# Output products, x and sums on halves of the array's columns between the transposes of batch 1's pairs

## Chip, cores, metric

One core of one Trainium2 chip. The metric is the device time of one execution in microseconds (us). All runs named here were with a granted clock (the share of TensorE's full clock) of 0.998 to 1.0. Engines: PE is TensorE, PEld its weight loads, ACT ScalarE, DVE VectorE, POOL GpSimd. A product has weights (lhsT, loaded by an instruction of its own) and a moving operand (rhs; in the trace of before, a whole-array product with 512 columns of it takes 0.216 us to the next one, with 288 columns 0.1225). P is the PSUM, in banks, where the products' results are written.

## The reference, cut to what matters

```python
# q, k, v: [8 batches, 8 heads, 576 tokens, 64]
kv = np.einsum('bhsd,bhse->bhde', k, v)
out = np.einsum('bhsd,bhde->bhse', q, kv)
rms = np.sqrt(np.mean(out * out, axis=-1, keepdims=True) + 1e-06)
x = out / rms * g_norm                  # then as [4608 tokens, 512]
y = ((x @ w_a) * (x @ w_b)) @ w_out     # w_a, w_b: 512 x 1536, w_out: 1536 x 512
```

## The kernel before

The heads go in pairs (64 + 64 rows). The tokens of the second stage go in strips of 512. While the output product of strip 0 runs (groups g = 0 to 3 of 128 tokens, 12 products of 512 columns each), the kernel prepares batch 1 in between: a piece of six products, then a step of each of the pairs that are under way. In the names, kv and qtr make the kv product and the transposes of q of a pair, x the product of q with it (`out` in the reference), psq its squares, pss the sums of these, and pst the normalized result. A product on a half uses 64 of the array's 128 columns (128\*64 in the profile's lines, where a whole one has 128\*128) and writes 64 output rows.

```python
def kv(self, p, o):                      # on halves: output rows 0-63 or 64-127
    for c, n in enumerate(rows):         # 6 for batch 1
        for j in range(2):
            nc.tensor.matmul(o[j * D : (j + 1) * D, :],
                lhsT=kk[0:n, 2 * p + j, c, :], rhs=vv[0:n, 2 * p + j, c, :], ...)

def qtr(self, p, i):                     # transposes, on halves too
    for c in range(EC):                  # 6
        for j in range(2):
            nc.tensor.transpose(t[j * D : (j + 1) * D, c, :],
                qt[self.b][:, 2 * p + j, c, :], ident[0:EP, 0:EP])
# ...
O, X, SS = 3, (4, 0), 6                  # PSUM banks; transposes and kv use bank 2
h1, h2 = range(0, FC // 2), range(FC // 2, FC)
ffn_o(0, 0, X[0])
pieces = [(1, h1), (1, h2), (2, h1), (2, h2), (3, h1), (3, h2)]
for n, (g, fcs) in enumerate(pieces):
    o_mm(0, g, O, fcs)                   # 6 products, full array
    if fcs is h2:
        o_out(0, g, O)                   # ACT or DVE copies bank O out
    if 0 <= n - 2 < NP:                  # NP = 4 pairs
        A.pss(n - 2, SS)                 # sums: 2 products, full array; then rs on ACT
        A.pst(n - 2, X[n % 2])           # DVE
    if 0 <= n - 1 < NP:
        A.x(n - 1, X[(n - 1) % 2])       # 2 products, full array
        A.psq(n - 1, X[(n - 1) % 2])     # square, ACT
    if n < NP:
        A.qtr(n, 2)
        A.kv1(n, 2)
        A.kv_out(n, P[:, 2, STRIP - D :])   # ACT
        A.qtr_out(n, 2)                     # DVE
```

## Time and profile before

| | kernel before |
|---|---|
| time | 315.76 us, median of 3 (315.75 to 315.96) |
| PE busy | 98% of the span |
| from the first transposes of batch 1 to the first product of strip 1 | 39.39 to 50.41 us: 11.02 us |

The last row is the stretch that the change touches, called "the stretch" from here on. It is read off the timeline, as the start of the first group of transposes and the start of the first group of products with wa_t after it.

### The profile page before, as it was taken

The numbers are of one execution on the slowest core, as the hardware profiler recorded it, in microseconds if no ns is written. First come the engines' busy times: TensorE is split into PE (matmuls) and PEld (weight loads), VectorE is DVE, ScalarE is ACT, GpSimd is POOL, SyncE is SP. The second block draws the span as 40 slices with busy tenths as digits, with TensorE's granted clock in tenths as the row PEclk, the third lists the DMA queues.
The fourth block names the chain that finished last, engine by engine and source line by source line (L and its number), as shares of the span: only waits on it lengthen the run. The fifth ranks groups of instructions, "written<-read, shape, count | busy, mean of one in ns | idle before, by whom it ended". The sixth has DMA issues, their size and how long they took to land.

```text
span 313.9 us, 4977 instructions
## 1 busy us (share of the span) xinstructions
PE 308.9 (98%) x1907; PEld 147.9 (47%) x1907; DVE 141.6 (45%) x235; ACT 115.9 (37%) x225; POOL 101.2 (32%) x123
## 2 busy tenths in 40 slices
PE   8999999999999999999999999999999999999995
PEld 3544454444445444544454445544544444444443
DVE  4544335456337703583377123761683134214321
ACT  3643255453246313451364024622651233123310
POOL 8954990282453730148138200320230000000000
PEclk9999999999999999999999999999999999999999
DMA  8999999999899999059999980073022200030002
GB/s 181 196 196 199 201 186 166 230 136 152 165 162 184 103 199 151 2 58 162 212 120 130 158 186 2 19 159 109 3 50 60 102 0 0 33 102 1 0 34 101
DMA packets 94253, 36.19 MB, mean 115 GB/s; under 512 B 64918, under 2 KB 89750, under 8 KB 94230
## 3 DMA queue, kind: packets, MB, share of 16 engines
q0 software_dynamic: 59120, 18.44, 54.3%
q1 hardware_dynamic: 34642, 16.87, 24.7%
q10 hardware_dynamic: 468, 0.57, 0.6%
q8 instruction: 15, 0.25, 0.3%
q14 instruction: 8, 0.07, 0.1%
HBM read 37.78 MB, written 12.98 MB: 162 GB/s over the span
## 4 chain that ended last, share of the span: by engine, by line
PE 98%; ACT 1%; issue 0%; DVE 0%
PE P L315 60%; PE P L372 30%; PE P L265 2%; PE P L400 2%; PE P L168 2%; PE P L192 1%; PE P L219 1%; PE P L206 0%; ACT sq L215 0%; PE P L245 0%; PE P L458 0%; ACT o_end L610 0%; PE P L462 0%; PE P L474 0%; DVE zeros L411 0%
## 5 line engine op out<-in xcount | busy, mean ns | idle before, releaser
L333 DVE TENSOR_TENSOR ab<-P,asb 128x512 bf16<-128x512 f32 x108 | 74.5, 691 | 103.6 <-PE P L315 86.0
L315 PE MATMUL P<-xt,wa_t 128*128 128x512 bf16 x432 | 111.9, 380 | 0.0
L315 PE MATMUL P<-xt,wb_t 128*128 128x512 bf16 x432 | 111.7, 379 | 0.0
L329 ACT CAST asb<-P 128x512 bf16<-128x512 f32 x108 | 63.0, 585 | 92.7 <-PE P L315 92.7
L372 PE MATMUL P<-wo_t,ab 128*128 128x512 bf16 (+1 forms) x444 | 95.8, 374 | 0.0
L372 PEld LDWEIGHTS <-ab 128*128 128x128 bf16 x444 | 43.0, 98 | 48.6
L315 PEld LDWEIGHTS <-wa_t 128*128 128x128 bf16 x432 | 41.4, 98 | 47.4 <-issue 0.2
L315 PEld LDWEIGHTS <-wb_t 128*128 128x128 bf16 x432 | 41.5, 98 | 46.9
L288 POOL TENSOR_TENSOR sqt<-rst,g_all 128x512 f32<-128x512 f32 (+1 forms) x24 | 25.0, 1043 | 96.2 <-ACT rst L281 96.2
L385 ACT COPY osb<-P 128x512 f32<-128x512 f32 x17 | 9.9, 585 | 67.3 <-PE P L372 57.5
L387 DVE COPY osb<-P 128x512 f32<-128x512 f32 x18 | 12.4, 691 | 44.1 <-PE P L372 39.5
L139 POOL DMA_DIRECT2D qs<-in_q_dram x12 | 19.8, 1653 | 0.7 <-issue 0.3
L276 DVE TENSOR_REDUCE sst<-sqt 128x8 f32<-128x512 f32 (+1 forms) x24 | 16.3, 680 | 1.8 <-ACT sqt L272 1.1
L297 DVE TENSOR_TENSOR qv<-P,sqt 128x512 bf16<-128x512 f32 (+1 forms) x24 | 16.4, 685 | 0.3
L272 ACT ACTIVATE sqt<-P 128x512 f32<-128x512 f32 (+1 forms) x24 | 14.4, 599 | 4.2 <-PE P L265 4.1
L265 PEld LDWEIGHTS <-qT 128*128 128x128 bf16 x120 | 9.2, 98 | 7.1
L265 PE MATMUL P<-kvb,qT 128*128 128x128 bf16 x120 | 11.6, 219 | 0.0
L281 ACT ACTIVATE rst<-sst,eps_t 128x8 f32<-128x8 f32 (+1 forms) x30 | 9.0, 300 | 4.6 <-DVE sst L276 4.3
L233 DVE SCALAR_TENSOR_TENSOR xt<-P,g_col,rs 128x288 bf16<-128x288 f32 x16 | 7.5, 512 | 5.2 <-ACT rs L223 5.2
L288 POOL TENSOR_TENSOR k_x<-rst,g_all 128x512 f32<-128x512 f32 x6 | 6.3, 1042 | 8.8 <-ACT rst L281 8.8
L131 POOL DMA_DIRECT2D wo_t<-in_moe_w_out_dram x12 | 6.4, 530 | 6.7 <-DMA wb_t<-in_moe_w_b_dram 3.2
L400 PE MATMUL P<-zeros 128*128 128x512 bf16 x17 | 7.2, 568 | 1.2 <-DVE eps_t L417 1.2
(67 smaller groups left out, 119.4 us busy)
## 6 DMA issues: line engine op xcount, KB each, us to landing
out_dram<-osb SPq DMA_DIRECT2D x23, 256.0 KB, 2.1
qs<-in_q_dram POOLq DMA_DIRECT2D x12, 288.0 KB, 7.0
ktl<-in_k_dram POOLq DMA_DIRECT2D x6, 512.0 KB, 9.2
vtl<-in_v_dram POOLq DMA_DIRECT2D x6, 512.0 KB, 11.9
out_dram<-osb SPq DMA_DIRECT2D x13, 128.0 KB, 2.4
wo_t<-in_moe_w_out_dram POOLq DMA_DIRECT2D x12, 128.0 KB, 6.0
wa_t<-in_moe_w_a_dram POOLq DMA_DIRECT2D x5, 256.0 KB, 9.0
wb_t<-in_moe_w_b_dram POOLq DMA_DIRECT2D x5, 256.0 KB, 9.6
```

Source lines behind the costliest of these rows:

```text
L139: nc.gpsimd.dma_start(out=d[:, hs, :], in_=q[b, hs].rearrange("h t d -> t h d"))
L265: nc.tensor.matmul(P[:, i, p * 128 : (p + 1) * 128], lhsT=self.qT[:, p, t0 : t0 + 128], rhs=kvb[self.b % 2][:, p, :], start=True, stop=True,)
L272: nc.scalar.activation(sqt[c % 3][r], self.by_head(i)[r], AF.Square)
L276: nc.vector.reduce_sum(sst[c % 3][r], sqt[c % 3][r], axis=mybir.AxisListType.X)
L288: nc.gpsimd.tensor_mul(sqt[c % 3][r], rst[c % 3][r].unsqueeze(2).to_broadcast([n, H, D]), g_all[r].unsqueeze(1).to_broadcast([n, H, D]),)
L297: nc.vector.tensor_mul(t[r], self.by_head(i)[r], sqt[c % 3][r])
L315: nc.tensor.matmul(self.a if w is wa_t else self.b, lhsT=w[:, kc, self.fc * 128 : (self.fc + 1) * 128], rhs=xt[:, kc, t0 : t0 + STRIP], st ...
L329: nc.scalar.copy(self.t, self.a)
L333: nc.vector.tensor_mul(abt[self.s % 2][self.fc], self.b, self.t)
L372: nc.tensor.matmul(P[:, i, e0:e1], lhsT=abt[s % 2][fc][:, g * 128 : (g + 1) * 128], rhs=wo_t[:, fc, e0:e1], start=(fc == 0), stop=(fc == F ...
L387: nc.vector.tensor_copy(t, P[:, i, :])
L400: nc.tensor.matmul(P[:, i, 0:cols], lhsT=zeros[:, 0:128], rhs=zeros[:, 0:cols], start=True, stop=True)
```

## The change

The intent: TensorE pays something each time it changes between the whole array and halves of its columns (0.09 us or a little more each way in this trace, as the prediction works out). The transposes and the kv products run on halves (their outputs are 64 rows). If the products between them run as two on halves as well, TensorE stays in halves from the first transposes to the last kv products.

```diff
+    def product(o, lhsT, rhs, halves=False, **kw):
+        for r in (slice(0, D), slice(D, 2 * D)) if halves else (slice(0, 2 * D),):
+            nc.tensor.matmul(o[r], lhsT=lhsT[:, r], rhs=rhs, **kw)
... (pss, x and o_mm call product and take halves)
     for n, (g, fcs) in enumerate(pieces):
-        o_mm(0, g, O, fcs)
+
+        halves = 0 < n < NP
+        o_mm(0, g, O, fcs, halves=halves)
...
-            A.pss(n - 2, SS)
+            A.pss(n - 2, SS, halves=halves)
...
-            A.x(n - 1, X[(n - 1) % 2])
+            A.x(n - 1, X[(n - 1) % 2], halves)
```

More of the change, by code (lines that the diff above doesn't have):

```diff
@@ L215, in psq, with pss @@
             nc.scalar.activation(sq[p % 3], P[:, i0 : i0 + 2, 0:HF], AF.Square)
-        def pss(self, p, i0, hs=(0, 1)):
+        def pss(self, p, i0, hs=(0, 1), halves=False):
             for h in hs:
-                nc.tensor.matmul(
-                    P[:, i0 + h, 0:HF], lhsT=ones, rhs=sq[p % 3][:, h, :], start=True, stop=True
+                product(
+                    P[:, i0 + h, 0:HF], ones, sq[p % 3][:, h, :], halves, start=True, stop=True
                 )
@@ L240, in pst, with x @@
                 )
-        def x(self, p, i0):
+        def x(self, p, i0, halves=False):
             for h in range(2):
-                nc.tensor.matmul(
+                product(
                     P[:, i0 + h, 0:HF],
-                    lhsT=kvb[self.b % 2][:, p, :],
-                    rhs=self.qT[:, p, h * HF : (h + 1) * HF],
+                    kvb[self.b % 2][:, p, :],
+                    self.qT[:, p, h * HF : (h + 1) * HF],
+                    halves,
                     start=True,
@@ L368, with o_mm @@
     n_o = [0]
-    def o_mm(s, g, i, fcs, e0=0, e1=d_model):
+    def o_mm(s, g, i, fcs, e0=0, e1=d_model, halves=False):
         for fc in fcs:
-            nc.tensor.matmul(
+            product(
                 P[:, i, e0:e1],
-                lhsT=abt[s % 2][fc][:, g * 128 : (g + 1) * 128],
-                rhs=wo_t[:, fc, e0:e1],
+                abt[s % 2][fc][:, g * 128 : (g + 1) * 128],
+                wo_t[:, fc, e0:e1],
+                halves,
                 start=(fc == 0),
```

## The prediction

> **What bounds the kernel now.** I read the page first: the busy shares and the chain that ended last. Both say that TensorE is the bound.
>
> ```profile
> PE 308.9 (98%) x1907; PEld 147.9 (47%) x1907; DVE 141.6 (45%) x235; ACT 115.9 (37%) x225; POOL 101.2 (32%) x123
> ...
> PE 98%; ACT 1%; issue 0%; DVE 0%
> ```
>
> The reader is to see that a TensorE stretch saved anywhere is saved at the end, unless another engine then makes TensorE wait. The list of waits bears this out: it shows no long TensorE wait after the first 16 us. So I went to the timeline of the stretch that the diff touches, about 39 to 51 us, where pieces of the output product (six 512-column products each) alternate with the preparation of batch 1's four pairs. The first column is the start of a group of products.
>
> ```profile
> 41.26 0.41 PE L245 MATMUL P<-qT,kvb 128*128 128x288 bf16 x2
> 41.60 0.45 PE L192 MATMUL P<-ident,qt 96*64 96x96 bf16 x12
> 41.88 0.35 PE L168 MATMUL P<-vt,kt 96*64 96x64 bf16 x12
> 42.16 1.47 PE L372 MATMUL P<-wo_t,ab 128*128 128x512 bf16 x6
> 43.47 0.41 PE L219 MATMUL P<-sq,ones 128*128 128x288 bf16 x2
> 43.72 0.41 PE L245 MATMUL P<-qT,kvb 128*128 128x288 bf16 x2
> 44.05 0.45 PE L192 MATMUL P<-ident,qt 96*64 96x96 bf16 x12
> 44.33 0.35 PE L168 MATMUL P<-vt,kt 96*64 96x64 bf16 x12
> 44.62 1.47 PE L372 MATMUL P<-wo_t,ab 128*128 128x512 bf16 x6
> 45.93 0.41 PE L219 MATMUL P<-sq,ones 128*128 128x288 bf16 x2
> 46.17 0.41 PE L245 MATMUL P<-qT,kvb 128*128 128x288 bf16 x2
> ...
> 60.86 0.82 PE L168 MATMUL P<-vtl,ktl 128*64 128x64 bf16 x40
> 61.62 0.61 PE L315 MATMUL P<-xt,wa_t 128*128 128x512 bf16 x2
> ```
>
> Two things are to be read from the starts. First, the switch. Two 288-column products take 0.245 us when another full-array product follows (43.47 to 43.72), but 0.33 to 0.34 when the half-array transposes follow (43.72 to 44.05, 41.26 to 41.60): 0.09 for going into halves. For coming out, take the half-array products of L168: 40 of them last 0.76 us to the next group, 12 of them 0.29 (44.33 to 44.62). The 28 more cost 0.47, which is 0.034 per pair, so 12 alone should take 0.20 and 0.09 is left for going back. In the single records of the trace the first group after each switch is also late by a little, 24 ns going in and 10 ns coming out, as its next weight load was not ahead. With those I count 0.117 in and 0.113 out, 0.23 for a round trip. Check: six at 0.216, 0.245 twice, 12 transposes at 0.255 and 12 products at 0.18 sum to 2.22, and the period from 42.16 to 44.62 is 2.46, so 0.24 is over.
>
> Second, halves run side by side. Twelve transposes of 96 columns take 0.28 us (41.60 to 41.88), that is 0.043 per pair after the first, while 96 columns alone need about 0.043 by the rate of the full products (512 in 0.216, 288 in 0.1225). In the single records the partner starts 3 ns later and the next pair 40 ns after that. The moving operand of both partners is the same identity, so reading one operand twice costs nothing there.
>
> [...] The trace has 110 ns for a 64-column load against 98 for a 128-column one. Under a product of 216 or 122 ns it stays hidden; even pairs of 64-column products follow each other every 32 ns.
>
> **The change part by part.** The order of TensorE's instructions was compared as built: 56 rows more, which is 28 weight loads and 28 products. They are 18 of the output product (three pieces of six, n = 1 to 3), 4 of the sums (n = 2, 3) and 6 of x (n = 1 to 3). ACT and DVE have as many instructions as before.
>
> What is removed: before, TensorE goes into halves and out again at each of n = 0 to 3, eight switches. After, it goes in before the transposes of pair 0 and out after the products of pair 3, two switches. Three round trips of 0.23 fall away: 0.69 us.
>
> What is added: 28 partners at about 3 ns, at most 0.08 us, and much less if the pairs overlap across their edges as the transposes do. I take 0.02.
>
> What comes back as waits: the period shrinks from 2.46 to 2.24, and ACT and DVE work between TensorE's steps has a fixed length. I followed it by record.
>
> ```profile
> 41.46 0.58 ACT L385 COPY osb<-P 128x512 f32<-128x512 f32 x1 [0.97 <-PE P L372]
> ...
> 43.92 0.74 ACT L223 ACTIVATE rs<-P,eps_t 128x576 f32<-128x576 f32 x1 [1.01 <-PE P L219]
> 44.55 0.64 ACT L215 ACTIVATE sq<-P 128x576 bf16<-128x576 f32 x1
> 45.09 0.41 ACT L179 CAST kvb<-P 64x64 bf16<-64x64 f32 x2
> ```
>
> ```profile
> 45.55 0.45 DVE L199 COPY qT<-P 128x576 bf16<-128x576 bf16 x1
> ```
>
> (a) The bank of the output product. At n = 1 a group ends and ACT copies it out; the next group (n = 2) writes the same bank and waits for ACT. The last product of the group starts at 41.26 - 0.216 = 41.045, the copy ends at 41.46 + 0.585 = 42.045, and a TensorE product waiting for ACT started 52 ns after ACT's end where I found one (9.465 to 9.517). So the next group can't start before 1.05 us after the last product of the group before. Now it comes at 42.165, 1.12 later, and just misses the wait. After the change TensorE gets there in 0.216 + 0.245 + 0.255 + 0.185 = 0.90. A wait of 0.15 us.
>
> (b) x(2) at n = 3. The sums of pair 0 start at 43.47; behind them ACT does rs, the square of pair 1 and the cast of kvb, then DVE copies qT, done at 46.00; with 52 ns that is 2.58 after the sums' start. TensorE takes 0.245 + 0.245 + 0.255 + 0.185 + 1.295 + 0.245 = 2.47 between the two after the change (2.70 before). A wait of 0.11 us.
>
> The other meetings keep room by the same reckoning: x(1) about 0.2 us (helped by wait (a)), x(3) about 0.1 us as the last switch out lies before it, the bank at n = 4 about 0.1. They are close, so a few hundredths may be wrong.
>
> Sum: 0.69 - 0.02 - 0.15 - 0.11 = 0.41 us gained on TensorE. Nothing behind the stretch seems able to take it back, since TensorE stays busy to the end and transfers wait for it rather than it for them. 315.76 - 0.41 = 315.35 us.
>
> **The rivals.** *Halves of long products run one after the other.* Then 18 x 0.216 + 10 x 0.1225 = 5.1 us come on top and the time is about 320.2, 1.4% slower. For it: no pair in this trace streams 512 columns, and both partners read the same 128 rows. Against it: the transposes share their moving operand too, and pairs of 288 columns on quarters (L206) start 3 ns apart. I give it 4%.
>
> *No wait takes anything back*, because ACT and DVE start earlier than I reckon: 0.67 gained, 315.1. For it: ACT's records overlap by about 0.1 us, so its sums are rough. Against it: each of the two waits hangs on one chain of operations without idle time between them.
>
> *The waits take all of it*, and TensorE is paced by ACT with a period of about 2.4: nothing gained, 315.7. For it: ACT does 0.74 + 0.64 + 0.42 and DVE 0.94 + 0.45 in a row in each period, and DVE's qT copy waits for ACT's cast. Against it: the longest loop is the 2.58 of (b), and it is set against a TensorE path of 2.47, not of 2.24.
>
> *Weight loads show*[...]: a few ns on each of 28 pairs, 0.1 to 0.2 us, so 315.5. Against it are the pairs of 64 columns every 32 ns.
>
> **Range and chances.** The repeated times lie within 0.2 us. The rivals that leave halves side by side span 315.1 to 315.7; with that noise I take 315.0 to 315.8. Two per cent would be 6.3 us, more than eight times all switches that go away, and more than halves one after the other would cost. So within 2% has 0.975, slower 0.015 (halves in sequence, with loads exposed as well), faster 0.01.
>
> **What would show each step right or wrong.** In the timeline after: groups of 12 products for the output at n = 1 to 3 that still take 1.3 us from their start to the next group (2.6 would be the first rival); no 0.09 between x and the transposes at n = 1, 2, 3, and none between the products of L168 and the output group at n = 0, 1, 2; one switch in and one out left. At n = 2 a gap of about 0.15 ahead of the output group, and at n = 3 about 0.1 ahead of x, both laid to ACT or DVE. The stretch from the first transposes to the first product of strip 1 (39.39 to 50.41, 11.02 us) should be about 10.6. The prediction is wrong if that stretch shrinks and the span doesn't, or if the long pairs have another pace than the short ones.

## More of the kernel before

As TensorE is busy to the end, what the stretch loses the span loses too, if nothing else steps in. Its ends, and the first kv products in it:

```profile
39.39 0.45 PE L192 MATMUL P<-ident,qt 96*64 96x96 bf16 x12
39.67 0.35 PE L168 MATMUL P<-vt,kt 96*64 96x64 bf16 x12
...
50.41 0.81 PE L315 MATMUL P<-xt,wa_t 128*128 128x512 bf16 x3
```

More lines of it are in the prediction.

## The result, and the profile after

| | median us | runs | mean us |
|---|---|---|---|
| before | 315.75 (315.67 to 316.1) | 6 | 315.83 |
| after | 315.57 (315.2 to 315.64) | 6 | 315.51 |

The ratio is 0.999, 95% interval 0.9977 to 1.0003. A ratio is the mean time of one kernel's runs over that of the other's of the same rounds, so it is not quite the ratio of the medians. The means differ by 0.32 us, less than the 0.41 forecast, and by the interval not clear of zero.

The chain that ended last was almost all TensorE before (98%). After, the profile's page shows another part in it (the second trace of the same kernel, after_again, has PE 94%, DMA 2%):

```profile
PE 86%; DMA 7%; POOL 4%; issue 1%; ACT 0%; POOLq 0%
```

The timeline of TensorE in the stretch, after. (All products made by the new helper are at L156. The transposes are L197 and the kv products L173.)

```profile
39.23 0.45 PE L197 MATMUL P<-ident,qt 96*64 96x96 bf16 x12
39.79 0.38 PE L173 MATMUL P<-vt,kt 96*64 96x64 bf16 x12
39.97 1.49 PE L156 MATMUL P<-wo_t,ab 128*64 128x512 bf16 x12
41.27 0.44 PE L156 MATMUL P<-qT,kvb 128*64 128x288 bf16 x4
41.52 0.45 PE L197 MATMUL P<-ident,qt 96*64 96x96 bf16 x12
42.01 0.38 PE L173 MATMUL P<-vt,kt 96*64 96x64 bf16 x12
42.19 1.49 PE L156 MATMUL P<-wo_t,ab 128*64 128x512 bf16 x12
...
43.98 0.45 PE L197 MATMUL P<-ident,qt 96*64 96x96 bf16 x12
44.24 0.38 PE L173 MATMUL P<-vt,kt 96*64 96x64 bf16 x12
44.43 1.49 PE L156 MATMUL P<-wo_t,ab 128*64 128x512 bf16 x12
45.73 0.44 PE L156 MATMUL P<-sq,ones 128*64 128x288 bf16 x4
46.10 0.44 PE L156 MATMUL P<-qT,kvb 128*64 128x288 bf16 x4
...
50.25 0.81 PE L321 MATMUL P<-xt,wa_t 128*128 128x512 bf16 x3
```

What is to be seen: twelve half products of 512 columns take 1.30 us to the next group, as six whole ones did. The switches are gone: x to transposes is 0.25 (41.27 to 41.52) where it was 0.34, and kv to the output group is 0.18 (42.01 to 42.19) where it was 0.28 or 0.29. But the transposes of pair 0 now last 0.56 to the kv products (39.23 to 39.79) and those of pair 1 last 0.49, where both took 0.28. That wait is not in the prediction. The chain of waits, cut to the same stretch in order of time, names it:

```profile
34.41 5.33 DMA vt<-in_v_dram
39.74 0.04 issue
39.79 0.38 PE P L173 x12
...
41.96 0.04 issue
42.01 0.38 PE P L173 x12
```

The kv products wait for the v rows of their pair: 34.41 + 5.33 = 39.74, and they start 0.04 later. The same landings, read from the records of the transfers, against the start of the kv products (us):

| kernel | pair 0: landed, started | pair 1 | pair 2 | pair 3 |
|---|---|---|---|---|
| before | 39.51, 39.67 | 41.73, 41.88 | 43.98, 44.33 | 46.17, 46.79 |
| after | 39.74, 39.79 | 41.96, 42.01 | 44.20, 44.24 | 46.40, 46.60 |

Before, the v rows had come 0.15 us ahead of their use for pairs 0 and 1, which leaves 0.11 to spare with the 0.04 from a landing to the start. The stretch after is 39.23 to 50.25, again 11.02 us in this trace. Its waits are 0.28 (v, pair 0), 0.24 (v, pair 1) and 0.12 (x at 46.10, predicted as 0.11), 0.64 in sum, about what the switches gave (0.69).

By the order of the program, the wait at pair 0 is not the change's doing: the first product that the change touches comes after the kv products of pair 0. Of the kernels below that alter nothing up to there either, halves_o waits there (39.33 to 39.76) and switch_more does not (39.47 to 39.75); of the kernel before there is one trace, without the wait. So the stretch mixes the change with a wait that comes and goes from trace to trace. From the first kv products to the first product of strip 1 the traces agree: before 10.74 (39.67 to 50.41; early_before too, 39.27 to 50.01), after 10.46 (39.79 to 50.25; after_again 39.75 to 50.21 and second_bank 39.64 to 50.10 too). That is 0.28 us gained. From there to the end of the span all ten traces take 263.52 to 263.55 us, so what is gained is kept. What the change meets is the wait at pair 1. Between the first two kv products no sums run, and TensorE needs 2.21 us before (39.67 to 41.88) and 1.99 after where nothing holds it (early_after, 39.58 to 41.56), but the v rows land 2.22 apart.

### The profile page after: what moved, and what is told of

Its sections match the earlier page's. It is cut to its first block, busy times and chain, and to the rows that moved or that the text cites. A ratio compares the mean times of both kernels' runs of the same rounds, so it can differ in the third digit from the quotient of the medians.

```text
span 313.8 us, 5034 instructions
## 1 busy us (share of the span) xinstructions
PE 308.6 (98%) x1935; PEld 149.0 (47%) x1935; DVE 141.5 (45%) x235; ACT 115.9 (37%) x225; POOL 101.2 (32%) x123
## 4 chain that ended last, share of the span: by engine, by line
PE 86%; DMA 7%; POOL 4%; issue 1%; ACT 0%; POOLq 0%
PE P L321 53%; PE P L156 29%; DMA wb_t<-in_moe_w_b_dram 6%; PE P L271 2%; PE P L173 2%; DMA vt<-in_v_dram 2%; POOL qt L116 1%; POOL wo_t L131 1%; POOL kt L116 1%; POOL vt L116 1%; POOL wa_t L441 0%; POOL wb_t L441 0%; PE P L197 0%; POOL wa_t L127 0%; ACT o_end L619 0%
## 5 line engine op out<-in xcount | busy, mean ns | idle before, releaser
L156 PE MATMUL P<-wo_t,ab 128*128 128x512 bf16 (+2 forms) x462 | 95.8, 374 | 0.0
L156 PEld LDWEIGHTS <-ab 128*128 128x128 bf16 (+1 forms) x462 | 43.7, 99 | 48.0
L184 ACT CAST kvb<-P 64x64 bf16<-64x64 f32 (+1 forms) x16 | 4.6, 285 | 10.5 <-PE P L173 10.4
```

The source lines that it names most:

```text
L156: nc.tensor.matmul(o[r], lhsT=lhsT[:, r], rhs=rhs, **kw)
```

## The experiments

Theory A: switches and halves cost what I said; what I left out is that batch 1's transfers land only just in time. They come one pair per 2.22 us, close to the new period of TensorE (2.24, and 1.99 from pair 0 to pair 1), and where they land varies by some 0.2 us from run to run. Theory B: only the two waits for ACT and DVE that I predicted count. The first four kernels ran on one chip and share nine runs of the kernel before (mean 315.80); the last four ran on another (nine runs, mean 315.81). Each has five timed runs and one trace. The 95% intervals of the ratios reach about 0.4 us to each side, so differences of 0.2 or 0.3 us in time are not clear of noise; the arguments rest on the traces.

### after_again: the changed kernel once more

> The changed kernel itself, once more. Theory A (transfers): in its first trace the products of L173 wait for the v rows of pairs 0 and 1 (the transfers landed at 39.744 and 41.964, the products began 42 ns later each time), and these landings move by some 0.2 us from run to run; so the gain varies with them. A expects the waits at pairs 0 to 2 again, each product group starting about 0.04 us after its landing, and 0.15 to 0.45 us gained. Theory B (the two waits that I predicted, for ACT and DVE, and no more) expects 0.4 us gained and a wait of 0.15 at the output group of n = 2.

Measured: correct; 315.65 us median, mean 315.61, 0.19 under before (ratio 0.9995, 0.9982 to 1.0007). Stretch 39.35 to 50.21, 10.86 us. v landed at 39.70, 41.92 and 44.18, and the kv products started at 39.75, 41.97 and 44.23. Waits: 0.12, 0.24 and 0.03 for v, 0.11 at x of n = 3; sum 0.50, against a stretch 0.16 shorter. So A holds for the landings: the products start 0.04 to 0.05 us after each again. The 0.16 by which the stretch differs from the first trace's is the wait at pair 0; from the first kv products on, both traces take 10.46. B's wait at the output group of n = 2 is not there (41.97 to 42.15, 0.18).

### early_before: transfers out of the way, kernel before

Two of the twelve tiles of w_out are not loaded, so what is behind them in the queue lands earlier (v by about 1.25 us, as measured below). The result is wrong.

```diff
-    for i in range(FC):
+    for i in range(FC - 2):
         load_o(i)
...
-                rhs=wo_t[:, fc, e0:e1],
+                rhs=wo_t[:, min(fc, FC - 3), e0:e1],
```

> The kernel before, with the last two of the twelve wo tiles not loaded and tile 9 used in their place (a wrong result on purpose): batch 1's q, k and v land about 1.3 us earlier. A: in the kernel before, every v landing had 0.15 us or more to spare, so the stretch from the first transposes of batch 1 to the first product of strip 1 stays 11.0 us and the time stays within 0.1 us of the kernel before, unless fewer loads help in the stretch ahead of it (up to 0.2). B expects the same.

Measured: 315.55 median, mean 315.55, 0.25 under before. v landed at 38.26, 40.48, 42.69 and 44.91, about 1.25 us earlier. The stretch is 38.99 to 50.01, 11.02 us: as before to the hundredth. So the transfers did not hold the kernel before in the stretch in its trace (in another execution they may at pair 0, as in halves_o). The time fell by a little more than the 0.2 I allowed; the stretch also began 0.4 us earlier in this trace than in that of before, but begins vary from 38.99 to 39.47 in these ten traces, so one trace does not settle that.

### early_after: transfers out of the way, changed kernel

The same edit on the changed kernel.

> The changed kernel with the same two loads left out (a wrong result on purpose). A: the waits for v are gone, the waits for ACT and DVE that I predicted take their place (0.15 at the output group of n = 2, 0.11 at x of n = 3), the stretch falls from 11.0 to about 10.6 us, and the time is 0.4 us under early_before. B: the same stretch as in the changed kernel, so no difference between early_after and after_again beyond that of early_before to the kernel before.

The timeline of TensorE in early_after:

```profile
41.56 0.35 PE L173 MATMUL P<-vt,kt 96*64 96x64 bf16 x12
41.91 1.49 PE L156 MATMUL P<-wo_t,ab 128*64 128x512 bf16 x12
...
45.43 0.44 PE L156 MATMUL P<-sq,ones 128*64 128x288 bf16 x4
45.82 0.44 PE L156 MATMUL P<-qT,kvb 128*64 128x288 bf16 x4
```

Measured: 315.25 median, mean 315.28, 0.27 under early_before. Stretch 39.30 to 49.97, 10.67 us. The kv products now follow the transposes with no wait. The wait that I had predicted at the output group of n = 2 is there: 0.35 from 41.56, of which the products need 0.185, so 0.165 (predicted 0.15). At x of n = 3 it is 0.39 - 0.245 = 0.145 (predicted 0.11). This is the stretch that I predicted (10.6), got by taking away the transfers that I had overlooked. So A holds for the stretch, and B, which expected the stretch of the changed kernel (11.02 and 10.86), falls. The time alone does not decide: 0.27 is less than the 0.4 that A expected, and the step from after_again (0.33) is only 0.08 more than that from the kernel before to early_before.

### early_short_copy: the bank comes free earlier

```diff
         t = o_sb[n % 4]
-        if n % 2:
+        if n == 1:
+            nc.scalar.copy(t[:, 0:128], P[:, i, 0:128])
+            nc.vector.tensor_copy(t[:, 128:], zeros[:, 128:])
+        elif n % 2:
             nc.scalar.copy(t, P[:, i, :])
```

> As early_after, and ACT copies only 128 of 512 columns out of the output bank at n = 1 (the rest of that row block is filled with zeros; wrong result on purpose), so that the bank comes free some 0.3 us earlier. If the wait at the output group of n = 2 is for this copy, it goes: the stretch is 0.15 us shorter than in early_after, about 10.45, unless x of the same n then waits longer for ACT's chain (at most 0.05). If that wait is for something else, nothing changes.

The timeline of TensorE in early_short_copy, at n = 1 and 2:

```profile
41.26 0.35 PE L173 MATMUL P<-vt,kt 96*64 96x64 bf16 x12
41.45 1.46 PE L156 MATMUL P<-wo_t,ab 128*64 128x512 bf16 x12
```

Measured: wrong result; 315.06 median, mean 315.00, 0.28 under early_after (more than the 0.17 by which the stretch shrank, but within the noise). ACT's copy took 0.27 us in place of 0.59. The output group follows the kv products after 0.19 us: the wait is gone. Stretch 38.99 to 49.49, 10.50 us, 0.17 less than in early_after. So that wait was for ACT's copy out of the bank. What is left is the wait at x of n = 3, 0.36 - 0.245 = 0.115. The stretch of before less 0.69, plus 0.115, would be 10.445; the 0.055 that is missing is what the partners and rounding take.

### halves_o: halves without fewer switches

The changed kernel, with halves for the output product alone:

```diff
-            A.pss(n - 2, SS, halves=halves)
+            A.pss(n - 2, SS)
...
-            A.x(n - 1, X[(n - 1) % 2], halves)
+            A.x(n - 1, X[(n - 1) % 2])
```

> The changed kernel with halves for the output product alone; the sums and x run on the full array again. TensorE then goes into and out of halves eight times, as in the kernel before, but in other places. If the gain is from switches alone and a pair of halves costs what one full product does, the stretch is 11.0 us as before (11.0 to 11.1) and the time within 0.1 us of the kernel before. If halving the long products gains or costs something by itself, the groups of 12 take other than 1.30 us.

Measured: correct; 315.86 median, mean 315.85, 0.04 over before (ratio 1.0002, 0.9989 to 1.0014). The groups of 12 take 1.40 to 1.42 to the next one, which is 1.30 and a switch of 0.1. Stretch 39.33 to 50.54, 11.21 us, longer than the 11.1 I allowed; 0.15 of the 0.19 is a wait for v at pair 0 (39.33 to 39.76, where 0.28 is usual), ahead of anything that was changed. Halving the products neither gains nor costs: the gain is in the switches.

### switch_more: 18 switches more

halves_o, with every second product of a group on halves:

```diff
-                halves,
+                halves and fc % 2 == 1,
                 start=(fc == 0),
```

> As halves_o, but in the output groups of n = 1 to 3 only every second product is in halves, so that each group has six switches more, 18 in all. If a switch costs 0.094 to 0.117 us here too, the stretch is 1.7 to 2.1 us longer than before (12.7 to 13.1) and the time 317.4 to 317.9. If switches between long products are hidden behind them, nothing changes.

The weight loads in switch_more, as groups in the timeline:

```profile
42.92 0.10 PEld L156 LDWEIGHTS <-ab 128*128 128x128 bf16 x1
43.24 0.11 PEld L156 LDWEIGHTS <-ab 128*64 128x64 bf16 x2 [0.23 <-issue]
43.58 0.10 PEld L156 LDWEIGHTS <-ab 128*128 128x128 bf16 x1 [0.23 <-issue]
```

Measured: correct; 317.84 median, mean 317.86, 2.05 over before (ratio 1.0065, 1.0053 to 1.0078). Stretch 39.47 to 52.53, 13.06 us, 2.04 more than before: 0.113 for each of the 18 switches. In the lines, the next load for the other kind comes 0.32 or 0.34 us after the last, where a product of 512 columns takes 0.216. So a switch costs 0.10 to 0.12 between long products too (0.117 and 0.113 in the prediction); all 18 show in the stretch.

### one_half_first: partners not next to each other

```diff
-        for fc in fcs:
-            product(... halves ...)
+        for r in (slice(0, D), slice(D, 2 * D)) if halves else (slice(0, 2 * D),):
+            for fc in fcs:
+                nc.tensor.matmul(P[r, i, e0:e1], lhsT=abt[...][:, r], ...)
```

> The changed kernel, with each output group of n = 1 to 3 ordered as six products on the first half of the columns and then six on the second, in place of partners in turn. If halves run side by side only where the next instruction is for the other half, each group takes 2.6 in place of 1.3 us, the waits of the changed kernel go, the stretch is about 14.3 us and the time about 319.0. If the engine finds partners further on in its queue, nothing changes against the changed kernel.

The timeline of TensorE in one_half_first, at n = 1:

```profile
39.89 1.49 PE L379 MATMUL P<-wo_t,ab 128*64 128x512 bf16 x10
41.19 0.29 PE L156 MATMUL P<-qT,kvb 128*64 128x288 bf16 x1
41.22 0.38 PE L379 MATMUL P<-wo_t,ab 128*64 128x512 bf16 x1
```

Measured: correct; 316.48 median, mean 316.48, 0.67 over before (ratio 1.0021, 1.0007 to 1.0035). Stretch 39.21 to 51.21, 12.00 us. Neither expectation holds. In the single records the first half's products start at 39.892, 40.113 and 40.328; the second half's first starts at 40.334, although three of the first half's, which stand before it in the program, have still to start. (The records do not name the half; the two rows of starts are told apart by their steps of 0.216 us.) So in this trace products further on in the program start while earlier ones have still to start, but not at once: the halves run 0.44 us out of step. x on the first half even starts (41.19) before the last two output products of the second half (41.22 and 41.44), which come before it in the program. The stretch is 1.1 us longer than in after_again, in place of the 3.9 of full sequence. Of the two orders, partners in turn is the better one here.

### second_bank: a correct version without the wait for the bank

```diff
-        o_mm(0, g, O, fcs, halves=halves)
+        bank = 7 if g == 1 else O
+        o_mm(0, g, bank, fcs, halves=halves)
         if fcs is h2:
-            o_out(0, g, O)
+            o_out(0, g, bank)
```

> The changed kernel with the output group of n = 0 and 1 in bank 7 (unused until n = 2), so that the group of n = 2 need not wait for ACT's copy; a correct version. By the theory that the v landings hold the stretch, nothing is gained as long as pair 1's v lands at about 41.95: the group of n = 2 starts 0.18 us after the products of pair 1, at most 0.05 us earlier than in the changed kernel, and the time stays within 0.1 us of it. By the theory that the bank is what counts, 0.15 us is gained.

The timeline of TensorE in second_bank, pair 1:

```profile
41.85 0.38 PE L173 MATMUL P<-vt,kt 96*64 96x64 bf16 x12
42.04 1.49 PE L156 MATMUL P<-wo_t,ab 128*64 128x512 bf16 x12
```

Measured: correct; 315.61 median, mean 315.59, 0.22 under before (ratio 0.9993, 0.9981 to 1.0006): the changed kernel's 0.19 to 0.32 again. Pair 1's v landed at 41.81 and the kv products started at 41.85. Stretch 39.27 to 50.10, 10.83 us. The output group follows after 0.19, against 0.18 in the changed kernel. Freeing the bank gains nothing while v comes that late. No version here beats the changed kernel clearly.

## Why the prediction was right, and where it was not

The time lies in the range (315.57, range 315.0 to 315.8; forecast 315.35), and the class "within 2%" was right. That shows little: the range also holds the kernel before (315.75), so no gain at all would have lain in it, and it is no proof of the mechanism. The stretch, which the prediction named as a sign, was 11.02 and 10.86 in place of about 10.6. By its steps:

- **Halves run side by side, long ones too.** Right: 1.30 us for 12, in all traces of the changed kernel. The first rival, halves one after the other, is out.
- **A switch costs 0.117 in and 0.113 out; three round trips make 0.69.** Right: 18 switches added cost 2.04 us, 0.113 each. With all but one of the waits away, early_short_copy's stretch is 0.52 shorter with 0.115 us of wait left: 0.64 of 0.69.
- **Partners cost 0.02.** About right; at most 0.06 by the same sum, for all 28.
- **The wait of 0.15 for the bank at n = 2.** The mechanism is right (0.165 in early_after, gone in early_short_copy), but in the changed kernel itself it does not appear, since pair 1's kv products wait for v just ahead of it and use the time up.
- **The wait of 0.11 at x of n = 3.** Its size is right: 0.12, 0.11 and 0.145. In the five traces with halves throughout and partners in turn, x starts 0.05 us after DVE's copy of qT ends (in the trace after, the copy ends at 46.05 and x starts at 46.10), as predicted. That the copy in turn hangs on the chain from the sums through ACT and DVE is argued from the records; no run removed it.
- **"Nothing behind the stretch seems able to take it back, since TensorE stays busy to the end and transfers wait for it rather than it for them."** This is the step that failed. Behind the stretch nothing does take it back (263.52 to 263.55 us in every trace). But in it TensorE waits for transfers: I did not check the loads that come into it. The kv products of pair 1 had 0.11 us to spare in the trace of before, and the change brings TensorE there 0.22 earlier. In the changed kernel they wait 0.24 for the v rows in both traces; this takes the place of the 0.15 for the bank and costs about 0.1 more. The wait at pair 0 (0.28 and 0.12) comes on top in these traces, but the change does not cause it.

So of 0.69 us, about 0.12 went to the ACT and DVE chain, as predicted, 0.24 to the transfers at pair 1, and some 0.05 to partners and rounding; 0.28 is left, where 0.41 was forecast. The means of the timed runs, 0.32 (6 against 6 runs), 0.19 (5 against 9) and 0.22 (second_bank), fit this, but do not show it by themselves: each interval of their ratios contains 1.

A limit stands behind this: v lands about once per 2.22 us at this point of the transfers' queue, and the period of TensorE after the change is 2.24, or 1.99 from pair 0 to pair 1. The transfers, TensorE and the ACT and DVE chain are about equally long there, so that taking one away shows the next: with the transfers out of the way, early_after has waits of 0.165 and 0.145 for ACT and DVE.

## What to carry to other kernels

When an engine is 98% busy, a shorter stretch of it still has to be checked against everything that enters the stretch: write the landing of each load beside the start of its first use, and compare what is to spare with what is gained ahead of that use. Where something ahead of the change varies from trace to trace, measure from a point behind it: here 0.28 us came out alike in three traces, while the stretch gave 0.00, 0.16 and 0.20. A change between whole array and column halves costs about 0.11 us in this kernel even between long products (0.113 for each of the 18 in switch_more), and doing the work between two half-array stages on halves as well removes it here for at most 0.06 us in all (28 partners, issued in turn; with each half's six in a row, in one_half_first, the stretch was 1.14 longer than in after_again). To see whether such a change works when another limit hides it, take the other limit away on purpose, even with a wrong result, and compare there.
